# A quarter of a weight moved to another DMA queue, a shorter road to block 5's input, and a conv slot moved to a border between matmul stages

## The chip, the core and the metric

The kernel runs on one core of one Trainium2 chip. The metric is the device time of one execution in microseconds (us), as the median of several executions. An execution that the hardware profiler recorded gives the trace: TensorE (PE, with its weight loads apart as PEld), VectorE (DVE), ScalarE (ACT), GpSimd (POOL) and SyncE (SP). ACT, POOL and SP also issue DMAs; POOL's go through the software queue q0, SP's through the hardware queue q1.

## The reference, cut to what matters

```python
# x: (8, 3904, 192), weight: (8 heads, 7 taps), float32
w = softmax(weight, axis=-1)
x_pad = concatenate([zeros((B, 6, D)), x], axis=1)
out = einsum('hk,bskhg->bshg', w, windows_of_7(x_pad))   # 24 channels a head
x = out.reshape(31232, 192)
a = x @ w1            # 192 x 1024
b = x @ w2            # 192 x 1024
h = (a * b) @ w3      # 1024 x 1024
return h @ w_out      # 1024 x 192
```

A causal convolution of seven taps, one set of taps a head, goes ahead of a feed-forward layer whose two first projections are multiplied with each other.

## The kernel before

The 31232 tokens are two streams of 15616 (`NS = 2`). A matmul of the first projections contracts over 64 of the 192 channels, and the two streams stand in the lower and the upper 64 partitions; so each weight is kept twice (`wd[0]` and `wd[1]`, partitions 0 to 63 and 64 to 127), and two matmuls on half of the array's rows each run side by side. `w3 @ w_out` is multiplied out on the core (`w3_product`, L464) to a 1024 x 192 matrix `W_sb`.

The convolution is a matmul with a band matrix (`band`, L245) over windows of 64 tokens, 58 of them new. The bands are made from `diag`, a matrix with a shifted diagonal that POOL makes with two selects out of a column of ones (L176), and from the softmax of the taps (L216 to L232). The windows are taken in 12 blocks of `SIZES = [6, 4, 8, 10, 8] + [36] * 6 + [20]` windows a stream. `conv` (L274) runs four 64 x 64 matmuls a head and leaves its result in PSUM; ACT or VectorE copies it to `convo` (L311). Blocks 0 to 4 are transposed on TensorE (L343, L507). From block 5 on, `store` (L316) writes the rows to DRAM, and SP's DMA transposes (L363) read them back into the ring `xT` of four rounds of 512 tokens.

The main loop (L579) goes by groups of four rounds. In a group there are first four `first_product` (L410), each of eight parts: a factor by `wd[0]`, a factor by `wd[1]` (six matmuls of 512 columns each, L381), a cast of the first factor to bf16 on ACT (L389), and the product of both on VectorE (L400). Then there are eight `second_product` (L420), 32 matmuls of 192 columns each, with two copies on ACT (L437) and one output DMA. Between second products stand the conv slots of a later block: `slots` (L572) are heads 0 to 2, 3 to 5, and 6 and 7, and the dictionary `at` (L590) says behind which second product, counted from 0, a slot stands. The last slot also stores its block on SP's queue. PSUM is four pairs of banks that are taken in turn (`banks`, L71).

All order is written out by hand: each engine runs its instructions, and each queue issues its DMAs, in the order of the program. At the start these stand around the change:

- ACT's queue: the DMA of the taps (`wall`, L137), a dummy exponential that loads the table (L157), the exponential of the taps, the cast of the first weight's first quarter into the lower half of `wd[0]`, two band copies (L479), the cast into the upper half of `wd[0]`, the cast into the lower half of `wd[1]` (all three from `wfirst`, L186), then copies of block 0's conv (L476).
- SP's queue: the first quarter of both weights as float32 into `wfirst` (L164).
- POOL's queue: block 0's x for stream 0 (L172), the two selects, block 0's x for stream 1, the first rows of each stream (L182), block 1's x (L119), the second quarter of both weights (L169, these DMAs cast to bf16), the cast of the second weight's first quarter into the upper half (L186), the third quarter, block 2's x, two copies of the second quarter to the upper half (L190), the last quarter, and so on with the copies and x of blocks 3 and 4.
- TensorE: six matmuls on zeros (L206), the taps' spread over the partitions (L230), two more on zeros, the bands (L256), conv of block 0, its transposes, conv of block 1, then the first parts of the first product.

Later POOL loads blocks 5 and 6 (L558). Ahead of that stands `pace` (L557), a copy of two elements of `w3T` that waits for a transpose of w3 on SP's queue (L461), so that the loads begin only then. `zero` (L562) clears the six rows ahead of a sequence's start after the block's load.

Of the kernel before, what the change touches and what calls it, by code (L numbers as in the profile page):

```python
# [8 lines left out]
FP32 = mybir.dt.float32  # L9
# [7 lines left out]
def kernel(  # L17
# [10 lines left out]
    nc = tc.nc  # L28
# [4 lines left out]
    DFF = moe_w1.shape[1]  # L33
    JT = DFF // 128
# [6 lines left out]
    GROUP = 4  # L41
    RING = GROUP * CH
    Q = 64
    ST = Q - PAD
    NP = D // Q
# [16 lines left out]
    work = ctx.enter_context(tc.tile_pool(name="work", bufs=2))  # L62
# [31 lines left out]
    def halves_of(b):  # L94
        n = SIZES[b] // 2
        return [(FIRST[b], 2 * n)] if 2 * n <= MAXN else [(FIRST[b], n), (FIRST[b] + n, n)]
# [8 lines left out]
    def load_x(b, parts=(0, 1)):  # L105
        tiles = xb_of.setdefault(b, [])
        zeros_of = zero_rows.setdefault(b, [])
        for i0, n in [v for e, v in enumerate(halves_of(b)) if e in parts]:
            xb = work.tile([128, n, D], BF16, tag="xb", bufs=5, name="xb")
            w = 0  # L110
            while w < n:
                i = i0 + w
                m = min(n - w, WB - i % WB)
                at_end = i + m == NWIN
                if at_end:
                    m -= 1
                if m:
                    for r in range(NS):
                        nc.gpsimd.dma_start(out=xb[Q * r:Q * r + Q, w:w + m, :],  # L119
                                            in_=x_spans(r, i, m))  # L120
                if i % WB == 0:
                    zeros_of += [(xb, 0, w), (xb, 1, w)]
                w += m
                if at_end:
                    nc.gpsimd.memset(xb[Q:128, w, :], 0.0)
                    t = tok(NWIN - 1) - PAD
                    nc.gpsimd.dma_start(out=xb[0:Q, w, :], in_=x_rows[t:t + Q, :])
                    nc.gpsimd.dma_start(out=xb[Q:Q + PAD + LAST, w, :],
                                        in_=x_rows[TS + t:TS + t + PAD + LAST, :])
                    w += 1  # L130
            if len(halves_of(b)) == 1:
                tiles += [(xb, 0), (xb, SIZES[b] // 2)]
            else:
                tiles.append((xb, 0))

    wall = const.tile([1, H, K], FP32)
    nc.scalar.dma_start(out=wall, in_=weight.rearrange("(o h) k -> o h k", o=1))  # L137

    n0 = SIZES[0] // 2
    xb0 = work.tile([128, 2 * n0, D], BF16, tag="xb", bufs=5, name="xb")  # L140
    xb_of[0] = [(xb0, 0), (xb0, n0)]
    wfirst = work.tile([Q, 2, NP, DFF // 4], FP32, tag="abT", bufs=GROUP, name="wfirst")
    pace = const.tile([1, 2], BF16)
    tiny = const.tile([128, 1], FP32)
    ones = const.tile([128, 1], BF16)
# [3 lines left out]
    diag = const.tile([128, Q + PAD], BF16)  # L149
    nc.vector.memset(zeros, 0.0)  # L150
    nc.vector.memset(tiny, 0.0)
    nc.vector.memset(ones, 1.0)  # L152
    nc.vector.memset(xb0[:, 0, :], 0.0)
    nc.vector.memset(half, 0.0)
    nc.vector.memset(half[:, Q:2 * Q], 1.0)
# [3 lines left out]
    WC = (0, DFF // 4, DFF // 2, DFF * 3 // 4, DFF)  # L159
    wd = [const.tile([128, NP, DFF], BF16, name=f"wd{i}", tag=f"wd{i}") for i in range(2)]  # L160
    w_rows = [w.rearrange("(k q) f -> q k f", q=Q) for w in (moe_w1, moe_w2)]

    for i in range(2):
        nc.sync.dma_start(out=wfirst[:, i], in_=w_rows[i][:, :, 0:WC[1]])  # L164

    def load_w(part):
        cs = slice(WC[part], WC[part + 1])
        for i in range(2):
            nc.gpsimd.dma_start(out=wd[i][0:Q, :, cs], in_=w_rows[i][:, :, cs])  # L169

    def load_x0(r):
        nc.gpsimd.dma_start(out=xb0[Q * r:Q * r + Q, 1:, :], in_=x_spans(r, 1, 2 * n0 - 1))  # L172

    load_x0(0)
    for p0 in (0, Q):
        nc.gpsimd.affine_select(  # L176
            out=diag[p0:p0 + Q], in_=ones[p0:p0 + Q].to_broadcast([Q, Q + PAD]),
            pattern=[[-1, Q + PAD]], compare_op=ALU.is_equal, fill=0.0, base=0,
            channel_multiplier=1)
    load_x0(1)  # L180
    for r in range(NS):
        nc.gpsimd.dma_start(out=xb0[Q * r + PAD:Q * r + Q, 0, :],  # L182
                            in_=x_rows[r * TS:r * TS + ST, :])
    load_x(1)
    def cast_w(i, r, f):
        f(out=wd[i][Q * r:Q * r + Q, :, 0:WC[1]], in_=wfirst[:, i])  # L186

    def copy_w(part, i, f):
        cs = slice(WC[part], WC[part + 1])
        f(out=wd[i][Q:128, :, cs], in_=wd[i][0:Q, :, cs])  # L190

    load_w(1)
    cast_w(1, 1, nc.gpsimd.tensor_copy)
    load_w(2)
    load_x(2)
    for i in range(2):
        copy_w(1, i, nc.gpsimd.tensor_copy)
# [5 lines left out]
    def warm(n):  # L203
        p, t = banks()
        for j in range(n):
            nc.tensor.matmul(t[:, j % 2, :], zeros, zeros[:, 0:1].to_broadcast([128, CH]),  # L206
                             start=True, stop=True)
        drained(p)

    warm(6)  # L210

    wmax = const.tile([1, H], FP32)
    wsum = const.tile([1, H], FP32)
# [4 lines left out]
        out=wall, in0=wall, in1=wmax.unsqueeze(2).to_broadcast([1, H, K]), op=ALU.subtract)  # L218
# [5 lines left out]
        out=wrow, in0=wall, in1=wsum.unsqueeze(2).to_broadcast([1, H, K]), op=ALU.mult)  # L224
# [228 lines left out]
    w3T = const.tile([128, JT, DFF], BF16)  # L453
# [19 lines left out]
    V, A, P = nc.vector.tensor_copy, nc.scalar.copy, nc.gpsimd.tensor_copy  # L473
# [4 lines left out]
    def put(f, p, dst, src):  # L478
        f(out=dst, in_=src)  # L479
        drained(p)  # L480

    cast_w(0, 0, A)
    put(A, *band(0, 0))
    put(A, *band(0, 1))
    cast_w(0, 1, A)
    made = [band(1, 0), band(1, 1)]
    put(V, *made[0])
    put(V, *made[1])
    cast_w(1, 0, A)

    def move_all(p, moves, fs):
        for f, m in zip(fs, moves):
# [41 lines left out]
    def need(R):  # L534
        return next(i for i in range(NWIN) if tok(i) >= (R + 1) * CH)
# [18 lines left out]
        3: seq([(pe_transposes, 4)])})  # L554
    store(4, need(GROUP - 1) - 1, queue=nc.gpsimd)
    nc.gpsimd.dma_start(out=wo_b, in_=wor)
    P(out=pace, in_=w3T[0:1, JT // 2 - 1, DFF - 2:DFF])  # L557
    load_x(5)  # L558
    load_x(6)
    first_product(3)  # L560
# [11 lines left out]
    slots = (range(0, 3), range(3, 6), range(6, H))  # L572
# [6 lines left out]
    for p, rounds in enumerate(groups):  # L579
        b = PROLOGUE_BLOCKS + p  # L580
        order = rounds[-1:] + rounds[:-1] if rounds[-1] == NR - 1 else rounds
        for j, R in enumerate(order if p else ()):
            first_product(R)
            send(R + GROUP)
            if j < 2 and b < NB:
                P(out=pace, in_=abT_of[R][0:1, JT - 1, 1, 0:2])  # L586
                load_x(b, (j,))
        if b < NB:
            zero(b)
        at = {1: [(b, slots[0])], 3: [(b, slots[1])], 5: [(b, slots[2])]}  # L590
        if p == 0:
            at = {0: [(5, slots[0], (V, A))], 1: [(5, slots[1], (V, A))],
                  2: [(5, slots[2], (V, A), need(GROUP))], 4: at[1], 5: at[3], 6: at[5]}
        for i, (R, r) in enumerate((R, r) for R in rounds for r in range(NS)):
            second_product(R, r, R == NR - 1 and r == 1, nc.sync if p else nc.gpsimd)
            for c in at.get(i, ()) if b < NB else ():
                conv_heads(*c)
            if p == 0 and i == 2:
                send(2 * GROUP - 1)
# [31 lines left out]
```

## Time and profile before

| | us |
|---|---|
| median of 3 executions | 521.86 (521.52 to 523.27) |
| the profiled execution | 522.07 |
| its span in the trace | 520.4 |
| TensorE busy | 513.5 |
| VectorE busy | 357.5 |
| ACT busy | 325.7 |
| POOL busy | 58.4 |

The profiled execution's own time is longer than the span, since the span goes from its first to its last recorded instruction. The granted TensorE clock was 1.00 throughout. Rows of the chain and of the timeline begin with a start in us from the span's start and a duration in us; in brackets stands how long the engine was idle ahead of it, and what released it. In the list of groups, the numbers behind the bar are the busy time in us, the mean of one in ns, and the idle time of the engine before them in us.

### The profile page before, as it was taken

Reading aid. Unit: us, or ns where it says so; the run is one execution under the profiler, and the core shown is the slowest. Engines: PE = TensorE matmul, PEld = TensorE weight load, DVE = VectorE, ACT = ScalarE, POOL = GpSimd, SP = SyncE. Lnnn points to the kernel's source line nnn. Section 1 sums busy time; section 2 is a strip of 40 time slices with the busy share of each in tenths; the row PEclk is TensorE's granted clock in tenths of the full one; section 3 lists DMA queues with packets and bytes.
Section 4 is the critical chain, followed back from the end, with each engine's and each line's share of the span. In section 5 each row is a group of like instructions: output and inputs, shape, how many; then the busy total and the mean of one; then the engine's idle time right before and its main releaser. Section 6 shows DMA issues by size and latency. Waiting matters only on the chain.

```text
span 520.4 us, 13006 instructions
## 1 busy us (share of the span) xinstructions
PE 513.5 (99%) x5576; PEld 339.8 (65%) x5576; DVE 357.5 (69%) x343; ACT 325.7 (63%) x410; POOL 58.4 (11%) x98
## 2 busy tenths in 40 slices
PE   8999999999999999999999999999999999999997
PEld 4455788455885558845588455884558855599567
DVE  6778646899538994389943899438993299911970
ACT  6887643777437774377743777337774377734762
POOL 8501522130000200002000010001200000000000
PEclk9999999999999999999999999999999999999999
DMA  9979998699656973569645699456724532024004
GB/s 116 169 142 126 163 222 208 162 186 166 143 146 161 116 94 113 146 161 128 82 116 147 155 122 89 118 146 157 103 44 122 155 96 32 17 94 151 1 3 152
DMA packets 133420, 64.61 MB, mean 124 GB/s; under 512 B 90304, under 2 KB 132642, under 8 KB 133298
## 3 DMA queue, kind: packets, MB, share of 16 engines
q1 hardware_dynamic: 94320, 44.06, 36.1%
q0 software_dynamic: 38896, 19.62, 30.4%
q8 instruction: 43, 0.70, 0.6%
q14 instruction: 15, 0.12, 0.1%
q10 hardware_dynamic: 146, 0.10, 0.1%
HBM read 33.25 MB, written 36.52 MB: 134 GB/s over the span
## 4 chain that ended last, share of the span: by engine, by line
PE 95%; ACT 1%; DVE 1%; DMA 1%; POOL 1%; issue 0%; POOLq 0%; ACTq 0%
PE pairs L381 59%; PE pairs L432 32%; PE pairs L290 3%; DVE abT L400 1%; PE pairs L467 1%; ACT asb L389 1%; DMA xb<-in_x_dram 1%; PE pairs L343 0%; POOL xb L172 0%; POOL xb L182 0%; ACT convo L311 0%; POOL xb L119 0%; ACT xT L355 0%; POOL diag L176 0%; PE pairs L507 0%
## 5 line engine op out<-in xcount | busy, mean ns | idle before, releaser
L400 DVE TENSOR_TENSOR abT<-asb,pairs 128x1024 bf16<-128x1024 bf16 (+1 forms) x245 | 298.1, 1217 | 76.8 <-ACT asb L389 60.5
L381 PE MATMUL pairs<-xT,wd 64*128 64x512 bf16 (+3 forms) x3000 | 319.7, 371 | 0.7 <-DVE abT L400 0.3
L389 ACT CAST asb<-pairs 128x1024 bf16<-128x1024 f32 (+1 forms) x245 | 247.1, 1009 | 67.7 <-PE pairs L381 67.3
L381 PEld LDWEIGHTS <-wd 64*128 64x128 bf16 x3000 | 162.3, 94 | 151.8 <-issue 1.8
L432 PE MATMUL pairs<-W_sb,abT 128*128 128x192 bf16 x1952 | 166.1, 246 | 0.0
L432 PEld LDWEIGHTS <-abT 128*128 128x128 bf16 x1952 | 159.6, 98 | 9.7 <-issue 9.7
L437 ACT COPY osb<-pairs 128x384 f32<-128x384 f32 x122 | 58.3, 478 | 116.0 <-PE pairs L432 116.0
L311 DVE CAST convo<-pairs 128x864 bf16<-128x864 f32 (+5 forms) x67 | 50.8, 815 | 67.6 <-PE pairs L290 67.6
L119 POOL DMA_DIRECT2D xb<-in_x_dram x42 | 32.2, 781 | 7.6 <-PE pairs L381 4.1
L586 POOL COPY pace<-abT 1x2 bf16<-1x2 bf16 x10 | 1.7, 174 | 238.7 <-DVE abT L400 238.7
L290 PE MATMUL pairs<-xb,Aband 64*64 64x432 bf16 (+5 forms) x384 | 17.5, 284 | 0.4 <-DMA xb<-in_x_dram 0.3
L290 PEld LDWEIGHTS <-Aband 64*64 64x64 bf16 x384 | 7.2, 106 | 7.5 <-issue 6.3
L311 ACT CAST convo<-pairs 128x512 bf16<-128x512 f32 (+4 forms) x15 | 8.1, 584 | 0.5 <-PE pairs L290 0.4
L444 POOL DMA_DIRECT2D out_dram<-osb x8 | 6.1, 758 | 18.4 <-ACT osb L437 18.4
L437 DVE COPY osb<-pairs 128x192 f32<-128x192 f32 x1 | 0.4, 358 | 11.1 <-PE pairs L432 11.1
L467 PEld LDWEIGHTS <-w3T 128*128 128x128 bf16 x64 | 5.2, 98 | 0.4 <-issue 0.4
L467 PE MATMUL pairs<-wo_b,w3T 128*128 128x192 bf16 x64 | 5.5, 246 | 0.0
L190 POOL COPY wd<-wd 64x768 bf16<-64x768 bf16 x6 | 4.8, 847 | 0.0
L206 PE MATMUL pairs<-zeros 128*128 128x512 bf16 x8 | 3.7, 615 | 1.1 <-DVE ones L152 1.1
L343 PE MATMUL pairs<-ident,convo 128*128 128x128 bf16 x48 | 3.9, 219 | 0.7 <-DVE convo L476 0.5
L343 PEld LDWEIGHTS <-convo 128*128 128x128 bf16 x48 | 2.9, 97 | 2.5 <-issue 1.6
L469 ACT CAST W_sb<-pairs 128x192 bf16<-128x192 f32 x8 | 2.6, 320 | 2.8 <-PE pairs L467 2.8
(52 smaller groups left out, 38.6 us busy)
## 6 DMA issues: line engine op xcount, KB each, us to landing
out_dram<-osb SPq DMA_DIRECT2D x52, 384.0 KB
xb<-in_x_dram POOLq DMA_DIRECT2D x18, 432.0 KB, 7.8
rows<-convo SPq DMA_DIRECT2D x8, 648.0 KB
out_dram<-osb POOLq DMA_DIRECT2D x8, 384.0 KB, 4.9
w3rows<-in_moe_w_dram POOLq DMA_DIRECT2D x2, 1024.0 KB, 12.0
xb<-in_x_dram POOLq DMA_DIRECT2D x6, 240.0 KB, 5.4
rows<-convo SPq DMA_DIRECT2D x4, 324.0 KB
xT<-rows SPq DMA_TRANSPOSE x81
```

The lines of the kernel that those rows point to most:

```text
L119: nc.gpsimd.dma_start(out=xb[Q * r:Q * r + Q, w:w + m, :], in_=x_spans(r, i, m))
L190: f(out=wd[i][Q:128, :, cs], in_=wd[i][0:Q, :, cs])
L290: nc.tensor.matmul(view(slice(Q * c, Q * c + Q), r)[:, :, j * G:(j + 1) * G], band_of(h, r), xb[Q * r:Q * r + Q, w0:w0 + n, h * G:(h + 1) ...
L311: f[e % len(f)](out=dst, in_=part)
L343: nc.tensor.transpose(out=tps[:, w, :], in_=convo[:, w, k].rearrange("p r g -> p (r g)"), identity=ident)
L381: nc.tensor.matmul(p[:, r, e * n:e * n + n], wd[i][rs, k, ft * 128:(ft + 1) * 128], xT[k][rs, r0 + c0:r0 + c1], start=(k == 0), stop=(k == ...
L389: nc.scalar.copy(out=asb, in_=pa)
L400: nc.vector.tensor_tensor(out=dst, in0=asb, in1=pb, op=ALU.mult)
L432: nc.tensor.matmul(ops[:, (g - g0) * D:(g - g0) * D + D], ab[:, jt, r, g * 128:(g + 1) * 128], W_sb[:, jt, :], start=(jt == 0), stop=(jt = ...
L437: f(out=osb[:, g0:g0 + per, :].rearrange("p g d -> p (g d)"), in_=ops[:, 0:per * D])
L444: queue.dma_start(out=out[t0:t0 + ng * 128, :].rearrange("(g p) d -> p g d", p=128), in_=osb)
L467: nc.tensor.matmul(wps[:, 0, 0:D], w3T[:, gt, jt * 128:(jt + 1) * 128], wo_b[:, gt, :], start=(gt == 0), stop=(gt == JT - 1))
```

## The change

At the start, the taps' DMA goes from ACT's queue to SP's, ahead of the weight. SP loads only the first weight's first quarter as float32; the second weight's first quarter is loaded by POOL, cast by the DMA, straight into the lower half of `wd[1]`, behind block 0's x and ahead of block 1's. Its upper half is then a copy on POOL from the lower half, behind the third quarter's DMAs. So ACT loses one cast, and POOL's cast becomes a copy. The column of ones is set by POOL instead of VectorE, and both selects stand ahead of all x. One warming matmul goes.

Later, `pace` waits for the second transpose of w3's second half instead of the fourth. In the loop, the third slot moves from behind second product 5 to behind second product 7 (in group 0, from 6 to 7), so that it stands between the last second product and the next group's first products; its two heads are copied by VectorE and ACT, one each, instead of both by VectorE.

```diff
-    nc.scalar.dma_start(out=wall, in_=weight.rearrange("(o h) k -> o h k", o=1))
+    nc.sync.dma_start(out=wall, in_=weight.rearrange("(o h) k -> o h k", o=1))
...
-    wfirst = work.tile([Q, 2, NP, DFF // 4], FP32, tag="abT", bufs=GROUP, name="wfirst")
+    wfirst = work.tile([Q, NP, DFF // 4], FP32, tag="abT", bufs=GROUP, name="wfirst")
...
-    nc.vector.memset(ones, 1.0)
...
-    for i in range(2):
-        nc.sync.dma_start(out=wfirst[:, i], in_=w_rows[i][:, :, 0:WC[1]])
-
-    def load_w(part):
+    nc.sync.dma_start(out=wfirst, in_=w_rows[0][:, :, 0:WC[1]])
+
+    def load_w(part, which=(0, 1)):
         cs = slice(WC[part], WC[part + 1])
-        for i in range(2):
+        for i in which:
             nc.gpsimd.dma_start(out=wd[i][0:Q, :, cs], in_=w_rows[i][:, :, cs])
...
-    load_x0(0)
+    nc.gpsimd.memset(ones, 1.0)
     for p0 in (0, Q):
         nc.gpsimd.affine_select(
...
+    load_x0(0)
     load_x0(1)
     for r in range(NS):
         nc.gpsimd.dma_start(out=xb0[Q * r + PAD:Q * r + Q, 0, :],
                             in_=x_rows[r * TS:r * TS + ST, :])
+    load_w(0, (1,))
     load_x(1)
-    def cast_w(i, r, f):
-        f(out=wd[i][Q * r:Q * r + Q, :, 0:WC[1]], in_=wfirst[:, i])
...
     load_w(1)
-    cast_w(1, 1, nc.gpsimd.tensor_copy)
     load_w(2)
+    copy_w(0, 1, nc.gpsimd.tensor_copy)
     load_x(2)
...
-    warm(6)
+    warm(5)
...
-    cast_w(0, 0, A)
+    A(out=wd[0][0:Q, :, 0:WC[1]], in_=wfirst)
     put(A, *band(0, 0))
     put(A, *band(0, 1))
-    cast_w(0, 1, A)
+    A(out=wd[0][Q:128, :, 0:WC[1]], in_=wfirst)
     made = [band(1, 0), band(1, 1)]
     put(V, *made[0])
     put(V, *made[1])
-    cast_w(1, 0, A)
...
-    P(out=pace, in_=w3T[0:1, JT // 2 - 1, DFF - 2:DFF])
+    P(out=pace, in_=w3T[0:1, 1, DFF - 2:DFF])
...
-        at = {1: [(b, slots[0])], 3: [(b, slots[1])], 5: [(b, slots[2])]}
+        at = {1: [(b, slots[0])], 3: [(b, slots[1])], 7: [(b, slots[2], (V, A))]}
         if p == 0:
             at = {0: [(5, slots[0], (V, A))], 1: [(5, slots[1], (V, A))],
-                  2: [(5, slots[2], (V, A), need(GROUP))], 4: at[1], 5: at[3], 6: at[5]}
+                  2: [(5, slots[2], (V, A), need(GROUP))], 4: at[1], 5: at[3], 7: at[7]}
```

## The prediction

> **What bounds the kernel now.** I read the page of the profile first, then the chain of work that ended last, window by window, then the timeline of the first 20 us and of one border between second and first products.
>
> ```profile
> span 520.4 us, 13006 instructions
> PE 513.5 (99%) x5576; PEld 339.8 (65%) x5576; DVE 357.5 (69%) x343; ACT 325.7 (63%) x410; POOL 58.4 (11%) x98
> PE 95%; ACT 1%; DVE 1%; DMA 1%; POOL 1%; issue 0%; POOLq 0%; ACTq 0%
> ```
>
> TensorE is the bound: 513.5 of 520.4 us busy and 95% of the chain. Only 6.9 us are not PE. So the change can gain in three ways: fewer PE microseconds per group, a shorter start, or the removal of a stray stall. All are small. The last 5% of the chain lies at the start:
>
> ```profile
> 1.32 0.85 POOL xb L172
> ...
> 2.26 0.28 POOL diag L176
> ...
> 2.85 0.65 POOL xb L172
> 3.50 1.09 POOL xb L182 x2
> 4.59 0.60 POOL xb L119
> 5.19 4.20 DMA xb<-in_x_dram
> ...
> 9.43 0.44 PE pairs L290 x31
> ```
>
> POOL issues block 0's x, the two selects, the rest of block 0's x, then block 1's x (L119). The second half of block 1's x is issued at 5.19 and lands at 9.39; conv of block 1 waits for it, and every first product stands behind that conv on PE's queue. **The issue time of block 1's x sets the start.**
>
> **Part 1, the start.** POOL's order becomes memset of ones, two selects, block 0's x, one weight DMA, block 1's x. Rows for the pieces:
>
> ```profile
> L169 POOL DMA_DIRECT2D wd<-in_moe_w_dram x6: 621/640/675, 5.8 to 12.7; - x6
> ```
>
> ```profile
> 0.42 0.10 POOL L615 MEMSET const-uint8-127<- 128x1 uint8 x1
> 0.82 1.40 SPq L164 DMA_DIRECT2D wfirst<-in_moe_w_dram  x2
> 0.90 0.11 DVE L150 MEMSET zeros<- 128x64 uint32 x1 [0.90 <-PEq L615]
> 1.32 0.85 POOL L172 DMA_DIRECT2D xb<-in_x_dram  x1 [0.80 <-POOLq L615]
> ```
>
> The selects only change place, so ahead of block 1's x POOL gains one weight DMA (0.64) and one memset (0.10): +0.74. Against this, POOL now sits idle from 0.52 to 1.32 while DVE computes from 0.90. If compute may start on POOL at 0.90 too, 0.42 of that idle time is filled, leaving +0.32. If the 0.80 is a fixed start, the full +0.74 stays. POOL's queue is free at the barrier like DVE's, so I lean to the first and take **+0.4** for block 1's issue.
>
> The transfer must carry the same load. DMA of the first 11 us:
>
> ```profile
> q0 software_dynamic: 2203, 0.88, 73.7%
> q1 hardware_dynamic: 416, 0.39, 13.6%
> ```
>
> A packet costs 0.737 x 11 x 16 / 2203 = 58.9 ns of an engine on POOL's queue and 0.136 x 11 x 16 / 416 = 57.5 ns on SP's. A quarter of a weight is 64 x 3 = 192 runs, so about 0.7 us of sixteen engines by either queue. Before, it competed with block 0's x; after, it is in front of block 1's x in one queue. Block 1's x has the same packets ahead of it, if the engines were busy all the time. Two bounds: 0 (all of it was ahead before) and +0.7 (it used to overtake nothing). I take 0, since the engines' share (the column before the last) was 1.19 from 3 to 9 us, so they had work throughout:
>
> ```profile
> 3.00:9.00 6.00, 4.96 (x160) 2.67 (x159) 5.07 (x15) 3.62 (x7) 5.96 (x10) 1.00 1.19 152
> ```
>
> So conv of block 1 starts at about 9.8 instead of 9.43: **+0.4 us on the path**, range -0.4 to +1.4. The lower end: if the data came in time, PE could go on at the end of block 0's transposes, 8.14 + 0.85 = 8.99 by the last row here, 0.44 sooner; the upper is +0.74 and +0.7.
>
> ```profile
> 4.45 0.83 ACT L186 CAST wd<-wfirst 64x768 bf16<-64x768 f32 x1 [1.46 <-DMA wfirst<-in_moe_w_dram]
> ...
> 5.38 0.27 ACT L479 CAST Aband<-pairs 128x128 bf16<-128x128 f32 x1
> ...
> 8.14 0.85 PE L343 MATMUL pairs<-ident,convo 128*128 128x128 bf16 x9 [0.55 <-DVE convo L476]
> ```
>
> The rest of this part is hidden. The weight row `wall` on SP pushes the first weight's DMA back by one issue (1.40/2 = 0.7), so ACT's cast may start at 5.15 and the first band copy at 6.0 instead of 5.38; ACT has 0.85 less to do after that (one cast of 0.83 goes), so it is level again before its next eviction. Cover: the wait for block 1's x until 9.8; without it, up to 0.6. One warm matmul fewer and VectorE's memset of ones shorten nothing that lasts: PE waits for the tap row behind the warm matmuls. The copy of the second weight on POOL (0.85, like L190's) now **waits for a DMA**, behind four more weight DMAs (2.56): with the shifted queue 6.2 + 2.56 = 8.8 to 9.7. Conv of block 1 takes 0.44 from 9.8, so the first product starts at 10.2 and its second factor, which reads the copy, some 0.4 later: 0.9 to spare. Queued behind it are block 2's x and six weight copies, all about 0.6 later; their readers, first products that start 0.4 later themselves, lose nothing if they had 0.2 of air; the chain of before goes through none of these copies.
>
> [...]
>
> **Part 2, the stall at block 5.** `pace` now looks at the second, not the fourth, transpose of the second half of w3, so POOL loads block 5 sooner.
>
> ```profile
> L461 SPq DMA_TRANSPOSE w3T<-w3rows x16: 1190/1261/5104, 26.8 to 52.7; - x16
> ```
>
> ```profile
> 51.22 0.17 POOL L557 COPY pace<-w3T 1x2 bf16<-1x2 bf16 x1 [9.60 <-DMA w3T<-w3rows]
> ...
> 67.45 0.25 POOL L564 MEMSET xb<- 6x192 bf16 x1 [0.34 <-DMA xb<-in_x_dram]
> ```
>
> ```profile
> 64.80 2.64 PE pairs L432 x32
> 67.44 0.30 PE pairs L290 x3
> ...
> 67.75 0.70 PE pairs L290 x9
> 68.46 2.75 PE pairs L432 x32
> 71.20 0.67 PE pairs L290 x12
> ```
>
> The memset of the rows before the sequence waits for block 5's data until 67.45 and ends at 67.70; PE's three heads took from 67.44 to 68.46, 1.02, against 0.67 in the next slot: 0.35 lost. Two transposes are 2 x 1.26 = 2.5 us; less the 0.6 that POOL is late, the loads start some 1.9 sooner. **-0.35** (bounds: 0, if the data is no sooner, and -0.35, since no more was lost).
>
> **Part 3, six borders.** The third slot (heads 6 and 7) goes from behind the sixth second product of a group to behind the eighth, in groups 0 to 5. Chain, group 1 and the end:
>
> ```profile
> 149.62 0.49 PE pairs L290 x8
> 150.10 5.39 PE pairs L432 x64
> 155.49 41.55 PE pairs L381 x384
> ```
>
> ```profile
> 456.11 21.23 PE pairs L432 x256
> 477.34 26.07 PE pairs L381 x288
> ```
>
> In group 0 a second product is 2.64 after w3's product and 2.75 after a conv: 0.11 more where the array's tile shape changes. First products (two row halves run as a pair): 192 pairs of 512 columns take 41.55; in the last group 96 pairs of 512 and 48 of 256 take 26.07. If a pair of 256 is half of one of 512, the difference, 15.48, is 72 pairs: 0.215 each, 41.28 for 192, and 0.27 is left at the entry. If each pair has a few ns of its own, less is left; the nearest row is the 0.11. A slot between two second products costs two changes; at the border the first product's entry is there anyway. So one of three changes goes: 6 x 0.11 = **-0.66**. Bounds: -1.3 if 64x64 to 64x128 were free, 0 if it cost double. Nearest row, a first product's part right behind conv:
>
> ```profile
> 19.30 1.40 PE pairs L381 x12
> ```
>
> 1.40 against 41.55/32 = 1.298 for a part: 0.10, one plain change. [...]
>
> What the move adds at the border: ACT and VectorE evict a head each ahead of the first products.
>
> ```profile
> L400 DVE TENSOR_TENSOR abT<-asb,pairs 128x1024 bf16<-128x1024 bf16 x242 | 295.5, 1221 | 75.7 <-ACT asb L389 59.5
> L311 ACT CAST convo<-pairs 128x864 bf16<-128x864 f32 x3 | 2.6, 879 | 0.4 <-PE pairs L290 0.4
> ```
>
> ```profile
> 155.53 0.48 ACT L437 COPY osb<-pairs 128x384 f32<-128x384 f32 x1 [0.80 <-PE pairs L432]
> 156.29 1.01 ACT L389 CAST asb<-pairs 128x1024 bf16<-128x1024 f32 x1 [0.28 <-PE pairs L381]
> 157.39 7.64 DVE L400 TENSOR_TENSOR abT<-asb,pairs 128x1024 bf16<-128x1024 bf16 x6 [5.39 <-ACT asb L389]
> ```
>
> From the last second product's end: ACT copies until 0.52, evicts head 7 until 1.42; the first factor is ready at 0.49 + 0.80 = 1.29, so the first cast is 0.13 late. Four bank pairs go round; the third part's second factor needs the pair that the first multiply frees. Now that is free at 157.39 + 1.22 - 155.49 = 3.12, and needed at 0.11 + 5 x 0.649 = 3.35: 0.23 to spare, 0.10 after. VectorE is done with head 6 long before. So 0 (bounds 0 and +0.65 a border: the whole 0.88 less 0.23). The store of the block moves 5.4 us on SP, to behind the two output stores; the transposes that read it follow a first product later and their data is read a whole group later: 0.
>
> **Sum:** +0.4 - 0.35 - 0.66 = -0.6. The profiled execution took 522.07 (span 520.4 and 1.67 around it), 0.2 above the median of 521.86; 521.47 for it, **521.3** for the median.
>
> **Rivals.** (a) Block 1's x lands 0.7 later still, behind the weight in its queue: +1.1 at the start, sum +0.1, **522.0**. For: one queue, in order; against: the engines were busy throughout. (b) The start gains: selects ride in POOL's idle 0.80, SP's second weight no longer shares the engines with x, conv starts at 8.99: -0.44 in place of +0.4, sum -1.45, **520.4**; with part 3 at its -1.3 it goes to 519.8. Against: the issue count above. (c) Slower: **the evictions at the border stall PE**. Price 0 to 0.65 each; above 0.1 a border the whole change loses, above 0.36 it loses over 0.3%. At 0.4: -0.6 + 2.4, **523.7**. It decides where the first cast is later than 0.23. For: VectorE's 7.64/6 = 1.27 a part leaves it 0.02 under PE's 1.298, so lateness is not caught up; against: the count of 0.13. (d) The change doesn't do what it says: the border's change costs double and block 5 still waits: +0.4, **522.3**.
>
> **Numbers.** Forecast 0.52, (a) 0.14, (b) 0.14, (c) 0.10, (d) 0.10. A measurement here tells some 0.3% (1.57 us) from no change. Under 520.3 lie (b) where part 3 goes further too, and the forecast's own edge, if part 1 costs nothing and part 3 brings 1.3 (521.86 - 1.65 = 520.2): faster 0.13. Above 523.4 lies most of (c) and a tail of (a): slower 0.10. Same 0.77. The range leaves out half of (c) and the edge of (b), 0.1 each: 520.0 to 523.2.
>
> **What would show it.** Conv of block 1 at 9.8 and waiting for DMA (right), at 9.0 (b), at 10.5 (a). Block 5's first three heads in 0.67 and `pace` near 49. Between groups: 5.28 in place of 5.39 for the last two second products, 0.49 for two heads, 41.55 for the first products; a longer one means (c), with PE waiting for L400 in the list of waits. Wrong would be any wait on VectorE in the groups, or a POOL start later than 1.8 for block 0's x.

## The result, and the profile after

The changed kernel took 524.04 us (median of 18 executions, 522.10 to 525.40), the kernel before 522.02 (18 executions, 521.12 to 523.27). The ratio is 1.0037, with a 95% interval of 1.0023 to 1.0050: **1.9 us slower** by the ratio (2.0 by the medians), where 0.6 us faster was forecast. The profiled execution of the changed kernel took 525.24, its span is 523.5; against the 520.4 of before it is 3.1 longer. Line numbers of the changed kernel are two or three lower (L379 is L381 of before, L288 is L290, L430 is L432).

The head of the page shows that TensorE's own work hardly grew, 514.0 against 513.5 us busy:

```profile
span 523.5 us, 13015 instructions
PE 514.0 (98%) x5575; PEld 347.2 (66%) x5575; DVE 351.5 (67%) x336; ACT 329.2 (63%) x415; POOL 59.1 (11%) x100
...
PE 94%; ACT 1%; DMA 1%; DVE 1%; POOL 1%; issue 0%; ACTq 0%; POOLq 0%
```

The chain of waits of the changed kernel, from the first issue to block 5's conv:

```profile
1.53 1.53 POOL xb L170 x2
3.06 1.07 POOL xb L181 x2
4.13 0.66 POOL wd L167
4.79 0.61 POOL xb L119
5.41 6.20 DMA xb<-in_x_dram
11.65 0.56 PE pairs L288 x27
...
47.24 15.81 PE pairs L379 x144
...
71.08 0.67 PE pairs L288 x12
```

The second half of block 1's x is issued at 5.41, 0.22 later than before, but its transfer takes 6.20 instead of 4.20: conv of block 1 starts at 11.65 instead of 9.43, 2.22 later. The long stretch of first products ahead of w3's product (144 matmuls) begins at 47.24; in the kernel before it begins 3.64 sooner, at 43.60. So another 1.42 us is lost between 12 and 47. Busy time by stretch (span of the stretch, then busy us and instruction count of PE, PEld, DVE, ACT and POOL, then the granted clock) shows where:

```profile
8.37:11.78 3.41, 0.41 (x21) 0.24 (x22) 0.29 (x1) 0.45 (x1) 2.30 (x4) 1.00 0.97 107
11.78:15.19 3.41, 3.41 (x53) 1.87 (x50) 1.57 (x3) 1.77 (x4) 3.15 (x5) 0.50 0.95 114
15.19:20.00 4.81, 4.81 (x68) 2.76 (x64) 3.06 (x5) 3.53 (x5) 4.81 (x8) 1.00 0.82 92
```

TensorE stands still from 8.65 to 11.65, and right behind that **its granted clock is halved for 3.41 us**, 11.78 to 15.19. Half of 3.41 is 1.7, near the 1.42; the first cast that the chain has behind this stretch begins at 18.84 instead of 15.22, so all but 0.02 of the 1.42 is lost by then. The 40-slice line of the page does not show it: there the slice reads 9 like all others. It can be seen in single matmuls too. TensorE's timeline at the start, the changed kernel and then the kernel before:

```profile
1.07 2.31 PE L204 MATMUL pairs<-zeros 128*128 128x512 bf16 x5 [1.07 <-DVE tiny L151]
3.53 0.21 PE L228 MATMUL pairs<-wrow,half 1*128 1x28 bf16 x2
...
11.65 0.56 PE L288 MATMUL pairs<-xb,Aband 64*64 64x48 bf16 x31 [3.00 <-DMA xb<-in_x_dram]
12.14 1.92 PE L379 MATMUL pairs<-xT,wd 64*128 64x348 bf16 x12
```

```profile
1.07 2.74 PE L206 MATMUL pairs<-zeros 128*128 128x512 bf16 x6 [1.07 <-DVE ones L152]
3.74 0.23 PE L230 MATMUL pairs<-wrow,half 1*128 1x28 bf16 x2
...
9.80 1.06 PE L381 MATMUL pairs<-xT,wd 64*128 64x348 bf16 x12
```

The same 12 matmuls take 1.92 at half clock and 1.06 at full clock. Note also the first two rows of each: six warming matmuls end as the tap row arrives, five end 0.15 us ahead of it (1.07 + 2.31 = 3.38, then nothing until 3.53).

The clock is not a matter of one execution. Each execution has a mean granted clock; a window of 3.41 us at half clock is 0.5 x 3.41 / 520 = 0.0033 of it. Of the 18 executions of the changed kernel 11 have a mean of 0.997 or 0.993 (one or two such windows) and take 523.60 to 525.40; four at 1.000 take 522.10 to 522.18, and the other three at 1.000 take 522.88 to 523.76 (experiment 10 shows a loss of clock that this mean misses). Of 117 executions of the kernel before, on the chips of the experiments below, 13 have 0.997 or less.

The other two parts show the durations that were forecast. Block 5's first heads take 0.67 (last row of the chain above), though part 2 was not the reason, as is shown below. At a border between groups:

```profile
147.43 10.67 PE pairs L430 x128
158.10 0.49 PE pairs L288 x8
158.59 41.64 PE pairs L379 x384
```

The last four second products take 10.67, where before 5.39 and 5.39 with a slot between them were needed: 0.11 saved. But the first products behind it take 41.64 instead of 41.55: **0.09 is given back**.

### The profile page after: what moved, and what is told of

Read it like the earlier page. It is cut to its first block, busy times and chain, and to the rows that moved or that the text cites. A ratio compares the mean times of both kernels' runs of the same rounds, so it can differ in the third digit from the quotient of the medians.

```text
span 523.5 us, 13015 instructions
## 1 busy us (share of the span) xinstructions
PE 514.0 (98%) x5575; PEld 347.2 (66%) x5575; DVE 351.5 (67%) x336; ACT 329.2 (63%) x415; POOL 59.1 (11%) x100
## 4 chain that ended last, share of the span: by engine, by line
PE 94%; ACT 1%; DMA 1%; DVE 1%; POOL 1%; issue 0%; ACTq 0%; POOLq 0%
PE pairs L379 59%; PE pairs L430 31%; PE pairs L288 3%; DMA xb<-in_x_dram 1%; DVE abT L398 1%; PE pairs L465 1%; ACT asb L387 1%; PE pairs L341 0%; POOL xb L170 0%; POOL xb L181 0%; ACT convo L309 0%; PE pairs L504 0%; POOL wd L167 0%; POOL xb L119 0%; ACT xT L353 0%
## 5 line engine op out<-in xcount | busy, mean ns | idle before, releaser
L379 PE MATMUL pairs<-xT,wd 64*128 64x512 bf16 (+3 forms) x3000 | 321.0, 372 | 0.7 <-DVE abT L398 0.2
L379 PEld LDWEIGHTS <-wd 64*128 64x128 bf16 x3000 | 169.4, 94 | 146.7 <-issue 3.9
L430 PEld LDWEIGHTS <-abT 128*128 128x128 bf16 x1952 | 159.9, 98 | 7.8 <-issue 7.8
L430 PE MATMUL pairs<-W_sb,abT 128*128 128x192 bf16 x1952 | 165.0, 246 | 0.0
L309 DVE CAST convo<-pairs 128x864 bf16<-128x864 f32 (+5 forms) x61 | 45.4, 798 | 96.7 <-PE pairs L288 96.7
L288 PE MATMUL pairs<-xb,Aband 64*64 64x432 bf16 (+5 forms) x384 | 17.3, 286 | 3.2 <-DMA xb<-in_x_dram 3.0
L288 PEld LDWEIGHTS <-Aband 64*64 64x64 bf16 x384 | 7.0, 107 | 10.2 <-issue 8.9
L309 ACT CAST convo<-pairs 128x864 bf16<-128x864 f32 (+5 forms) x21 | 13.1, 653 | 0.4
L167 POOL DMA_DIRECT2D wd<-in_moe_w_dram x7 | 4.4, 650 | 0.0
```

Source lines behind the costliest of these rows:

```text
L288: nc.tensor.matmul(view(slice(Q * c, Q * c + Q), r)[:, :, j * G:(j + 1) * G], band_of(h, r), xb[Q * r:Q * r + Q, w0:w0 + n, h * G:(h + 1) ...
L309: f[e % len(f)](out=dst, in_=part)
L379: nc.tensor.matmul(p[:, r, e * n:e * n + n], wd[i][rs, k, ft * 128:(ft + 1) * 128], xT[k][rs, r0 + c0:r0 + c1], start=(k == 0), stop=(k == ...
L430: nc.tensor.matmul(ops[:, (g - g0) * D:(g - g0) * D + D], ab[:, jt, r, g * 128:(g + 1) * 128], W_sb[:, jt, :], start=(jt == 0), stop=(jt = ...
```

## The experiments

After the result I held these theories of the late start. **F**: one instruction fetch is slow on one of the 16 DMA engines that carry block 1's x, and the wait halves the clock. **O**: the order of POOL's queue, the weight ahead of x. **G**: an engine lags for a reason of its own. **L**: the loop's edits, not the start. After experiment 8 two more stood against each other: **W**, TensorE's clock, which one warming matmul fewer and idle time at the start make rise late or fall; and **X**, the wait for x alone. Each ratio is to the kernel before on the same chip, with its 95% interval.

**1. The start alone** (the changed kernel with the loop and `pace` of before).

```diff
-    P(out=pace, in_=w3T[0:1, 1, DFF - 2:DFF])
+    P(out=pace, in_=w3T[0:1, JT // 2 - 1, DFF - 2:DFF])
...
-        at = {1: [(b, slots[0])], 3: [(b, slots[1])], 7: [(b, slots[2], (V, A))]}
+        at = {1: [(b, slots[0])], 3: [(b, slots[1])], 5: [(b, slots[2])]}
...
```

> The changed start alone, pace and the third slot as before. Theory F (in the start, one DMA engine serves a 16 KB instruction fetch of PE amid a full POOL queue, so its share of block 1's x lands up to 3 us late, and PE's wait then halves its clock for 3.4 us): all of the loss and a little more, +2.4 against before, median near 524.4, in more than half of the executions a mean clock of 0.997 or less. Theory L (the loss is in the loop, by the evictions at the border): no change against before, 522.0 within 0.5.

Measured: 523.24 (12 executions, 521.91 to 525.91), before 522.51, ratio 1.0014 [0.9994, 1.0033]. The profiled execution is the fastest of the twelve: block 1's x lands at 9.43 there, and the clock stays. Four of 12 take over 524.5. So the start has a tail, and the profile of one execution can miss it.

**2. The loop alone** (the kernel before with the new `pace` and the new third slot).

```diff
-    P(out=pace, in_=w3T[0:1, JT // 2 - 1, DFF - 2:DFF])
+    P(out=pace, in_=w3T[0:1, 1, DFF - 2:DFF])
...
-        at = {1: [(b, slots[0])], 3: [(b, slots[1])], 5: [(b, slots[2])]}
+        at = {1: [(b, slots[0])], 3: [(b, slots[1])], 7: [(b, slots[2], (V, A))]}
...
```

> The start of before with the changed pace and third slot. Theory F: the gains alone, -0.35 for block 5's wait and -0.2 for six borders: 521.4, every clock at 1.000. Theory L: +2.0, 524.0, with the clock at 1.000.

Measured: 521.98 (521.09 to 522.71), ratio 0.9981 [0.9966, 0.9995]: faster by 1.0 us by the ratio (the medians differ by 0.5), so L falls. But its list of waits of TensorE, and POOL's timeline, show a new one:

```profile
PE pairs L467 <- DMA w3T<-w3rows: 1.3, 1, 1.3
```

```profile
49.56 6.20 POOL L119 DMA_DIRECT2D xb<-in_x_dram  x8 [0.36 <-PE pairs L381]
```

Block 5's loads start at 49.56 (51.75 before), beside the last transposes of w3, and w3's product waits 1.3 us for one of these. That the loads held it back was not tested by itself. In the changed kernel TensorE is 3.6 us later there, and the wait does not appear.

**3. The weight behind block 1's x** instead of ahead of it.

```diff
-    load_w(0, (1,))
     load_x(1)
+    load_w(0, (1,))
```

> The changed kernel, but the second weight's first quarter is issued behind block 1's x instead of ahead of it. Block 1's x is issued 0.65 sooner, at 4.1 and 4.75, and is mostly through when PE's second instruction fetch comes at 7.5. Theory F: block 1's x lands by 8.5, the clock stays at 1.000, 520.9. Theory O (only the weight's own transfer in front of x costs: 0.7 us on the engines): 0.7 better than the changed kernel, 523.3, and the clock still falls in half of the executions.

Measured: 524.20 (521.84 to 525.96), ratio 1.0027 [1.0007, 1.0047]. Two of TensorE's waits, the stretch with the first of them, and the one behind:

```profile
PE pairs L379 <- DMA wd<-in_moe_w_dram: 1.0, 1, 1.0
PE pairs L379 <- POOL wd L188: 0.6, 1, 0.6
```

```profile
7.57:10.98 3.41, 2.10 (x52) 1.24 (x48) 1.72 (x5) 2.31 (x5) 1.17 (x3) 1.00 1.11 134
10.98:17.81 6.83, 6.27 (x54) 3.79 (x55) 2.76 (x4) 2.05 (x4) 6.83 (x10) 0.50 0.82 95
```

Now x is in time (it lands at 8.36) and the first products wait for the weight and its copy, and the clock is halved for 6.83 us. The order of the two in POOL's queue only chooses which one is late; O alone does not explain the loss.

**4. The weight on SP as before**, with the taps on ACT's queue, six warming matmuls, the selects ahead of x, and the changed loop and `pace`.

```diff
-    nc.sync.dma_start(out=wfirst, in_=w_rows[0][:, :, 0:WC[1]])
+    for i in range(2):
+        nc.sync.dma_start(out=wfirst[:, i], in_=w_rows[i][:, :, 0:WC[1]])
...
-    load_w(0, (1,))
...
-    warm(5)
+    warm(6)
...
+    cast_w(1, 0, A)
```

> The selects in front, pace and third slot as changed, but the second weight's first quarter is loaded by SP as float32 and cast by ACT and POOL as before, and the taps by ACT. POOL's queue holds one weight DMA less. Theory F: block 1's x is issued at 4.1 and 4.75 and lands by 8.8; 521.0, clock at 1.000. If moving the selects alone brings the loss (an earlier start of all that makes PE's fetch meet the x of block 1): as the changed kernel, 524.0.

Measured: 522.57 (521.29 to 523.52), ratio 1.0001 [0.9985, 1.0018]; profiled 521.46, span 519.8. Conv of block 1 does not wait for x (it lands at 8.30). Nothing of the tail above 523.6 is left, but half of the executions still have a mean clock of 0.996 to 0.997, and the loop's gain does not show in the median.

**5. The changed kernel again**, to see whether the result repeats on another chip.

> The changed kernel itself once more, as the anchor beside the others. Both theories: 1.004 of before, a mean clock of 0.997 or less in about half of the executions.

Measured: 524.73 (7 executions, 522.81 to 525.71), ratio 1.0041 [1.0022, 1.0059]: it repeats. Here x lands at 9.91, near the 9.8 that was forecast, and TensorE waits only 0.88 for it, from 9.07 on; yet the clock is halved from 9.21 to 16.04:

```profile
5.79:9.21 3.42, 2.22 (x101) 1.53 (x98) 2.52 (x7) 2.09 (x6) 3.38 (x6) 1.00 1.15 128
9.21:16.04 6.83, 6.09 (x79) 3.87 (x80) 2.50 (x4) 2.91 (x7) 6.83 (x11) 0.50 1.10 127
```

Of the wait for block 1's x only 0.14 lies ahead of the fall; the longer gaps there are 0.32 (for block 0's x) and 0.61 (for VectorE's copy of block 0's conv). So a long wait for block 1's x is not needed for the loss. F loses weight; W and X were formed on this.

**6. TensorE kept busy** ahead of block 1's conv.

```diff
+    warm(8)
     move_all(*conv(1, 0, H, "streams"), (A, V))
```

> The changed kernel with eight matmuls on zeros ahead of conv of block 1, so that TensorE works 1.7 us of its wait. Theory F (late x, and on top a halved clock because TensorE waits): the clock stays at 0.999 or more in nearly every execution, the slow executions come down by 1 to 1.7 us, the best ones lose up to 1.2: median 523.2. If the halved clock has nothing to do with the wait: clocks as in the changed kernel, median 524.5.

Measured: 523.00 (522.64 to 525.11; ten of 12 within 522.64 to 523.41), ratio 1.0022 [1.0009, 1.0034], against 524.73 for the unchanged kernel on the same chip, whose interval overlaps with this one. The filling matmuls push conv itself back, and the median still falls by 1.7. The profiled execution is the worst of the twelve, 525.11: the filling matmuls run at 3.19/7 = 0.456 each, where 11 has 1.03/4 = 0.26 at a granted clock of 1.00; that the clock had not risen by 12.6 is read from this.

```profile
9.48 3.19 PE L204 MATMUL pairs<-zeros 128*128 128x512 bf16 x7 [0.22 <-issue]
12.61 0.44 PE L288 MATMUL pairs<-xb,Aband 64*64 64x48 bf16 x32
```

**7. Conv of block 1 ahead of block 0's transposes**, with three warming matmuls, to get the instruction fetch behind the landing of x.

```diff
-    warm(5)
+    warm(3)
...
+    move_all(*conv(1, 0, H, "streams"), (A, V))
...
-    move_all(*conv(1, 0, H, "streams"), (A, V))
```

> The changed kernel with conv of block 1 ahead of block 0's transposes and two warming matmuls fewer, so that PE is blocked by its wait for block 1's x before it reaches the instruction at which it fetched 16 KB more (about the 309th). Theory F (the fetch on one DMA engine makes block 1's x late): the fetch begins only after that x has landed, it lands by 8.9, and the slow executions go: 522.8, since the transposes stand 0.9 later. Rival G (one DMA engine of the sixteen lags for another reason, the queue of weight DMAs itself): x lands as late as before, 525.

Measured: 524.71 (6 executions, 523.17 to 525.35), ratio 1.0047 [1.0030, 1.0065]. The fetch did not move behind the landing: it begins between 8.6 and 9.0, while x is under way. But it took only 0.89 us, and x still landed at 10.77, one of its 16 shares 1.85 behind the others; a fetch of 0.89 does not account for that. The experiment is not clean in another way too: with three warming matmuls TensorE waits 1.06 us for the tap row, and its clock first rises at 15.1 by the trace's clock record.

```profile
PE pairs L288 <- DMA xb<-in_x_dram: 3.0, 3, 2.0
...
PE pairs L228 <- DVE wrow L221: 1.1, 1, 1.1
```

**8. The border done otherwise**: the kernel before with the third slot at the border, VectorE taking the last copy of the eighth second product, ACT head 6 and VectorE head 7.

```diff
...
-            f = nc.vector.tensor_copy if last and g0 == 0 else nc.scalar.copy
+            f = (nc.vector.tensor_copy if last and g0 == 0 or border and g0 + per == ng
+                 else nc.scalar.copy)
...
+        at = {1: [(b, slots[0])], 3: [(b, slots[1])], 7: [(b, slots[2], (A, V))]}
...
+            second_product(R, r, R == NR - 1 and r == 1, nc.sync if p else nc.gpsimd,
+                           i == 7 and b < NB)
```

> Before, with the third slot at the border alone (start and pace as before); VectorE copies the last pair of the last second product, ACT head 6, VectorE head 7. If the 0.09 that the first products of groups 1 to 3 gained is the bank pair that the first multiply frees too late, ACT's first cast is now on time and they take 41.55 instead of 41.64: 0.11 saved at each of six borders, -0.66 against before. If it is the entry from the 64 by 64 tiles: still 41.64, -0.2.

Measured: 521.35 (520.72 to 522.22), ratio 0.9983 [0.9970, 0.9997], **faster than both kernels** on its chip (the changed one took 524.73 there, in 5). Experiments 12 and 13 contain the same edit, and their intervals include no change. Chain at the border:

```profile
144.17 10.67 PE pairs L432 x128
154.84 0.49 PE pairs L290 x8
155.32 41.55 PE pairs L381 x384
```

41.55 again, so the whole 0.11 stays. Why the changed kernel gives 0.09 back is seen by setting both timelines of the border side by side, first the changed kernel's, then this one's:

```profile
158.52 3.13 PEld L379 LDWEIGHTS <-wd 64*128 64x128 bf16 x31 [0.34 <-issue]
...
159.47 1.02 ACT L387 CAST asb<-pairs 128x1024 bf16<-128x1024 f32 x1
160.57 3.67 DVE L398 TENSOR_TENSOR abT<-asb,pairs 128x1024 bf16<-128x1024 bf16 x3 [0.99 <-ACT asb L387]
...
161.85 3.13 PEld L379 LDWEIGHTS <-wd 64*128 64x128 bf16 x31 [0.20 <-issue]
```

```profile
155.25 5.72 PEld L381 LDWEIGHTS <-wd 64*128 64x128 bf16 x55 [0.34 <-issue]
...
157.22 3.76 DVE L400 TENSOR_TENSOR abT<-asb,pairs 128x1024 bf16<-128x1024 bf16 x3 [0.67 <-ACT asb L389]
```

From the first products' start to the first multiply it is 160.57 - 158.59 = 1.98 in the one and 157.22 - 155.32 = 1.90 in the other (and 1.90 in the kernel before). In the changed kernel the weight loads stop for 0.20 and go on at 161.85, just behind the end of the first multiply (160.57 + 1.22 = 161.79), which frees the bank pair that the third part's second factor writes. In the other kernel they run through. The profile names no releaser for the 0.20 ("issue"); that it is the bank pair is read from these times.

**9. The changed kernel with six warming matmuls.**

```diff
-    warm(5)
+    warm(6)
```

> The changed kernel with six warming matmuls as before instead of five. Theory W (the loss is the clock: with five, PE stands still ahead of the tap row at 3.4 to 3.8, and its clock rises a window of 3.4 us later or falls again): the clock rises by 6 in most executions, 523.0, at least 1 us less than the changed kernel's 524.4. Theory X (the wait for block 1's x alone decides, by its late engine): as the changed kernel, 524.4.

Measured: 522.38 (521.49 to 525.65), before 522.22, ratio 1.0012 [0.9990, 1.0034]. Eight of 12 executions lie at 522.74 or below; the other four, at 524.37 to 525.65, have a mean clock of 0.997 or 0.993. In the profiled execution TensorE waits 0.86 for x, and the 12 matmuls behind it take their full-clock time:

```profile
9.94 0.44 PE L288 MATMUL pairs<-xb,Aband 64*64 64x48 bf16 x31 [0.86 <-DMA xb<-in_x_dram]
10.30 1.06 PE L379 MATMUL pairs<-xT,wd 64*128 64x348 bf16 x12
```

The stretch with that wait is as idle as the one ahead of the fall in 5, 2.20 us busy against 2.22, and the clock holds behind it:

```profile
7.74:11.16 3.42, 2.20 (x53) 1.46 (x53) 1.79 (x5) 1.74 (x5) 3.38 (x6) 1.00 1.12 134
```

By the ratios, 1.0012 and 1.0037, one matmul of 0.46 us is worth 1.3 us. But the intervals of this kernel and of the changed one overlap, because the four remain.

**10. The kernel before with five warming matmuls**, the mirror of 9.

```diff
-    warm(6)
+    warm(5)
```

> Before with five warming matmuls instead of six, nothing else. Theory W: slower than before by 0.5 to 1.5, since in some executions the clock rises late; theory X: as before, 522.2.

Measured: 523.06 (521.24 to 523.46; nine of 12 in 522.76 to 523.46), ratio 1.0015 [1.0004, 1.0025]: one matmul fewer costs 0.8 us, with nothing else changed. In the profiled execution block 1's x is in time and the clock rises late:

```profile
3.75 0.21 PE L230 MATMUL pairs<-wrow,half 1*128 1x28 bf16 x2 [0.36 <-DVE wrow L223]
...
9.84 1.92 PE L381 MATMUL pairs<-xT,wd 64*128 64x348 bf16 x12
```

1.92 instead of 1.06 at 9.84, without any wait for x: X cannot give that. The mean clock of all these executions reads 1.000, since it is counted from the first recorded change, which comes at 13.4 here: **a late rise does not show in the mean**, only in the durations.

**11. The changed kernel with seven, and four more ahead of block 1's conv.**

```diff
-    warm(5)
+    warm(7)
...
+    warm(4)
     move_all(*conv(1, 0, H, "streams"), (A, V))
```

> The changed kernel with seven warming matmuls at the start and four more ahead of conv of block 1. Theory W: every clock at 0.999 or more after an early rise, no execution above 523.5, median 522.3. Theory X: late x stays, a third of the executions above 524.

Measured: 522.43 (522.38 to 523.62; eleven of 12 within 522.38 to 522.76), ratio 1.0010 [1.0001, 1.0018], an interval wholly below the changed kernel's. All executions but one agree within 0.4 us: the tail is gone.

```profile
9.00 1.03 PE L204 MATMUL pairs<-zeros 128*128 128x512 bf16 x4
...
10.33 1.06 PE L379 MATMUL pairs<-xT,wd 64*128 64x348 bf16 x12
```

**12. The border of 8, with block 5's loads sooner.** The edit of 8, and:

```diff
-    P(out=pace, in_=w3T[0:1, JT // 2 - 1, DFF - 2:DFF])
+    P(out=pace, in_=w3T[0:1, 2, DFF - 2:DFF])
```

> The best so far (start of before, third slot at the border with VectorE on the last copy) and pace on the third transpose of w3's second half instead of the fourth. If block 5's x then comes 1.3 us sooner and w3's transposes still end ahead of their product: 0.35 better than with the old pace, 521.0; if the loads hold back w3's transposes, as when pace stood on the second: the same or worse, 521.4 or more.

Measured: 521.66 (520.85 to 522.87), ratio 0.9992 [0.9982, 1.0002]. In the profiled execution (span 519.1) TensorE waits nowhere from 43.15 to 71.07, and block 5's heads take 0.67; the median is no better than that of 8. The 0.35 of part 2 could not be shown as a gain in time.

**13. The border of 8, with two more matmuls** between block 0's conv and its transposes.

```diff
+    warm(2)
```

> The start of before, the third slot at the border with VectorE on the last copy, and two matmuls on zeros between block 0's conv and its transposes, where PE stands still for 0.5 us. Theory W (a fuller TensorE in the first 10 us keeps the clock): as the same kernel without them at its best, 520.9 to 521.4, no execution above 522. If the spread of before has another cause: median 521.4 and as wide as without.

Measured: 521.89 (520.61 to 524.24), before 521.72, ratio 0.9997 [0.9983, 1.0010]. No gain: the spread stays, and in the profiled execution TensorE waits 0.9 at block 5, whose data comes only at 68.61 here. W had forecast no execution above 522; five of 12 are.

**14. The changed kernel with six, and the two of 13.**

```diff
-    warm(5)
+    warm(6)
...
+    warm(2)
```

> The changed kernel with six warming matmuls and the two matmuls on zeros between block 0's conv and its transposes. Theory W alone: no execution above 523, median 521.7. Theory W and a late x of its own (block 1's x behind the weight on POOL's queue): still a quarter of the executions above 524 with a mean clock of 0.997, median 522.3.

Measured: 522.25 (521.37 to 524.68; two of 12 above 524), before 521.72, ratio 1.0013 [0.9999, 1.0026]. The mean effect is that of experiment 9, with fewer executions in the tail (two instead of four, too few to call it a difference). W alone (none above 523) fails here too; the two above 524, with a mean clock of 0.997, are what W with a late x of its own forecast, at 522.3.

## Why the prediction was wrong

**The step that failed is part 1's price of the start: +0.4 for block 1's x, and nothing for the clock.** The clock was put at nothing by "One warm matmul fewer and VectorE's memset of ones shorten nothing that lasts". The row behind that was right, TensorE does wait for the tap row. But the warming matmul did something besides filling time: it kept TensorE running up to that row. Without it (10) the kernel before loses 0.8 us (0.2 to 1.3 by the interval); with it again (9) the changed kernel's ratio is 1.0012 instead of 1.0037, with intervals that overlap. Matmuls that only fill the start thin the tail out (6) or end it (11) though they add work. The clock is shown as the means by the halved window of the profile after, by the pairs at 1.92 in 10, and by the mean clock of the executions. In the profile after itself the missing matmul was not the cause: by the trace's clock record the clock had risen at 4.95 there, and it fell behind the wait of 3.00 for x.

The clock of "1.00 throughout" that stands ahead of the prediction holds only from 4.61 on, where the clock record of the profile before begins; until then its warming matmuls take 2.74/6 = 0.46 each, against 1.03/4 = 0.26 in 11 at a granted clock of 1.00.

The halved stretches lasted 3.41 us (the profile after) and twice that, 6.83 (3 and 5); the first rise of the 16 profiled executions lies anywhere from 3.79 to 15.11 by the traces' clock records. The loss is small against a span, 1.42 of 523.5 us in the profile after: but 0.4% is all that there was to win or lose here. Nor does it take a long gap: in 5 the clock fell behind gaps of 0.61 us and less.

How much idle time is too much can be narrowed down by windows of 3.41 us counted from the clock's changes; that the clock is decided once in such a window is an estimate of mine, from the changes in the profile after at 4.95, 11.78 and 15.19, which lie 6.83 and 3.41 apart. In the window ahead of a fall TensorE was busy for 0.41 us (the profile after), 2.10 (3) and 2.22 (5); in windows of the start behind which the clock held, for 2.20 (9, the row there), 2.42 (4) and more. So at this start the border lies near 2.2 busy us of 3.41, an estimate from these. The first rises at 4.29 (1), 4.61 (the profile before) and 4.95 (the profile after) lie less than a window apart, so by that estimate the windows begin at another point of the kernel in each execution, and the same gaps fall into one window or into two; that would let one kernel have executions with the loss and without it, but this was not tested. Busy time alone is not the rule, though: in 2 the clock held behind a window with 2.07 at w3's product (60.33 to 63.74), and at the end of 5, where second products run, behind one with 1.48:

```profile
517.79:521.21 3.42, 1.48 (x18) 1.25 (x16) 0.36 (x1) 0.80 (x2) 0.00 (x0) 1.00 0.70 230
521.21:523.10 1.89, 0.00 (x0) 0.00 (x0) 0.00 (x0) 0.00 (x0) 0.00 (x0) 1.00 0.00 0
```

For the first rise no such border shows: it came behind a window with 3.02 busy in 1, and not behind windows with 3.05 and 3.03 in 10.

**Part 1, the arrival of x: too small.** POOL began at 0.82 and issued the second half of block 1's x at 5.41, 0.22 later than before where 0.4 was forecast. What was mis-sized is the transfer, which was to take as long as before: 6.20 instead of 4.20 in the profile after. Landing was taken as 9.39 plus 0.4. In the profiled executions of the eight kernels with the weight on POOL's queue ahead of x it landed at 8.84, 9.16, 9.43, 9.62, 9.89, 9.91, 10.77 and 11.60; in the seven with the weight on SP at 8.30, 8.50, 8.74, 8.76, 8.82, 9.35 and 9.39. Each of these is one execution of one kernel. The medians are 9.76 and 8.76. So 9.8 was right as a landing, but the 9.39 it was compared with was the latest of its kind, and the difference is 1.0, not 0.4; the part of it behind 8.99, where the prediction has TensorE free, costs time, 0.8. The range's upper end of +1.4 was passed in the profiled execution (+2.22). Rival (a) had this direction and was priced at 0.7 by the packets; it did not price the clock behind the wait, 1.42 in the profile after.

Why one of the 16 engines' shares came 2.9 us behind the others in the profile after **stays open**. F had this row for it: q8 (instruction fetches) in the DMA view of 6 to 8 us, first the changed kernel, then the kernel before, with the share of 16 engines' time last:

```profile
q8 instruction: 1, 0.02, 9.0%
```

```profile
q8 instruction: 1, 0.02, 3.0%
```

That is 0.09 x 2 x 16 = 2.9 us for one fetch, against 0.95. It fits the 2.9, but in 7 a share lagged by 1.85 with a fetch of 0.89, so a fetch as slow as that is not needed, and in 10 the last share came 0.20 behind with a fetch of 1.5. The traces do not name the engine of a share. G cannot be told from the queue's own order by these runs.

**Part 2: the 0.67 came as forecast, but by luck.** POOL's rows of the profile after:

```profile
51.99 0.17 POOL L554 COPY pace<-w3T 1x2 bf16<-1x2 bf16 x1 [6.73 <-DMA w3T<-w3rows]
52.53 6.20 POOL L119 DMA_DIRECT2D xb<-in_x_dram  x8 [0.36 <-PE pairs L379]
...
69.30 0.25 POOL L561 MEMSET xb<- 6x192 bf16 x1 [0.33 <-DMA xb<-in_x_dram]
```

`pace` stood at 51.99 and not near 49, the loads began later than before (52.53 against 51.75) and so did the memset behind their data (69.30 against 67.45). TensorE did not wait because it came there 3.64 later itself, at 71.08 instead of 67.44. In 2, with the start of before, the loads did begin 2.2 sooner, but the memset came only 0.13 sooner, at 67.32, and TensorE found it done only because it had lost 1.3 to w3 ahead of it. In 4, with the new `pace` and TensorE in time, the heads took 0.96. In 1, with the old `pace`, the memset came at 66.95 and the heads took 0.67 too. So the start of the loads does not by itself set when block 5's data is there; what does stays open. In time the part was not shown to gain (12).

**Part 3: the switch was right, the slack was not.** 0.11 a border was forecast and measured (8 keeps it whole). "0.23 to spare, 0.10 after" failed: the need was taken as the third part's matmul at 3.35, but its **weight load** comes ahead of it and, by the times in 8, waits for the bank pair too, so with a multiply 0.08 later the first products behind the six borders took 41.56, 41.64, 41.64, 41.64, 41.59 and 41.55 instead of 41.55 each: 0.32 of the 0.66 is lost again. That is rival (c)'s mechanism at a seventh of its upper price of 0.65 at most. It takes half of the gain, but it does not make the kernel slower.

Sum, by the profiled executions: +2.22 (x) + 1.42 (clock) - 0.35 (block 5) - 0.66 + 0.32 (borders) = +2.95; the spans differ by 3.1, so 0.1 to 0.2 is left over. The 0.35 stands there as a duration, not as a gain of the new `pace`. For all executions, by the ratios: the loop alone gave -1.0 us (2), one warming matmul +0.8 on the kernel before (10), the start in all +0.7 with a wide interval (1). These do not add up to the +1.9 of the whole except at the ends of their intervals; whether the parts strengthen each other was not settled.

## What to carry to other kernels

Price the idle time of a short matmul kernel's start twice, as the time itself and as what it does to the granted clock behind it (here 2.22 us and 1.42 us, in the profile after); matmuls that only fill a gap may be worth more than their own time (11 has 1.0010 where the changed kernel has 1.0037). Look at the executions one by one: a tail that is in 11 of 18 executions moves the median, and one profiled execution says nothing of it. When a wait goes as forecast, look whether its own cause went, or whether the engine that waited came late. When a slack of a tenth of a us is counted, count it to the weight load, not to the matmul (here the weight loads stood still for 0.20 us).

The best version here is experiment 8: the start left alone, the slot at the border, and the last copy ahead of it on VectorE (0.9983 [0.9970, 0.9997]). With small additions (12, 13) its gain was not clear of the noise.

## What the runs showed of the hardware

- In the profiled executions the granted clock knew two values, 1.00 and 0.50, and a fall at the start lasted 3.41 us (the profile after) or 6.83 (3, 5); at half clock the 12 matmuls of a first part took 1.92 instead of 1.06.
- In the first 12 us the clock fell behind windows of 3.41 us with 2.22 us or less of busy TensorE (the profile after, 3, 5), and held behind windows with 2.20 (9), 2.42 (4) and more.
- A gap of 0.36 us ahead of the tap row went with a clock that rose at 13.4 by the trace's clock record (10), where the kernel before, without a gap, has 4.6; but with gaps of 0.15 and 0.20 it had risen at 4.95 (the profile after) and 4.29 (1), so a gap alone does not decide it.
- The mean clock of an execution misses a late first rise: all executions of 10 read 1.000.
- The 16 shares of one transfer do not land together: 15 of 16 were there at 8.71, the last at 11.60, in the profile after.
